# A planner's transfer times, the places of its loads, and a lag: one re-plan of a fused attention and FFN kernel

## The chip, the cores and the metric

The kernel runs on one core of a Trainium2 chip. The metric is the device time of one launch in microseconds. TensorE (PE), VectorE (DVE), ScalarE (ACT) and GpSimd (POOL) compute; SyncE (SP) issues most of the DMAs, POOL those of the FFN weights.

## What is computed

Forgetting attention for 8 batches of 8 heads (576 tokens, head size 64), and a SwiGLU block on its output. All inputs and the output are float32; the kernel computes its matrix products in bf16.

```python
scores = scale * np.matmul(q, k.transpose(0, 1, 3, 2))
cum = np.cumsum(np.log(np.clip(f, 0.0001, 1.0)), axis=-1)
decay = cum[:, :, :, None] - cum[:, :, None, :]
scores = np.where(causal, -1000000000.0, scores + decay)
attn = softmax(scores)
x = np.matmul(attn, v)          # to tokens x 512
g = x @ w_gate                  # 512 x 1536
out = (g * sigmoid(g) * (x @ w_val)) @ w_out
```

## The kernel before, in words

**Work.** Attention goes by pairs of heads: 32 pairs, four to a batch. A pair's queries come in nine blocks of 64 rows. Blocks 0 to 3 are group g = 0, blocks 4 to 8 are g = 1. For each pair: k and q are loaded (L325; two slots each, kf and qf), cast to bf16 on POOL (kb at L352, qb at L350), transposed on PE (L364) into one of two PSUM banks "tx", and copied out by ACT or DVE (L378, L380) to kt and qz. The cumulated log gates of the two heads, cb, are loaded from DRAM (L332, five slots). PE makes the scores in one of two banks "sp" (L399, with a mask at L403), DVE adds cb and takes the row minimum (L415), ACT takes exp with the row sum (L429), DVE inverts the sums (L445, L447; ACT may do the first step, L443), and POOL normalizes into the packed tile pk (L464). Then P is transposed into pT: for pairs 0 to 7 on PE (L488, with copies out at L493), for pairs 8 to 31 by a transposing DMA issued by SP (L476): one of 19 blocks for g = 1, one of 6 for g = 0. P times V (L514) goes to a "tx" bank, and ACT or DVE copies it into xT (L538), a ring of 2560 tokens.

**FFN.** Tokens go in tiles of 256, 256, seven times 512, 256, 256. Per tile and unit of 512 columns: gate and value products (L595, banks "gv"), tanh on ACT (L601), two DVE operations (L603, L606) to hh. Then the output product (L620; one bank "op"; in groups of four matmuls, three groups for 128 tokens), its eviction to ot by ACT (L630) or DVE (L632), and the store (L637).

**What sets the order.** Nothing is ordered by hand. The code makes a list of operations, each with the engines that may run it and a cost in ns on each, what it reads and writes, a due time `prio`, and for a DMA its transfer time `dma`. `Plan.order` then runs a list scheduler on this model: again and again it takes the operation that can start first (ties: smaller `prio`), on the engine where this holds, and books the engine. It gives one fixed order for each engine; on the chip every queue runs in that order, and each instruction waits for its own data and buffers. A wrong cost gives no wrong result, but an order that doesn't fit. Three things matter here:

- *Due times.* `ORDER` numbers the units (pair, group): first the eight of pairs 0 to 3, then two for each later pair, g = 1 before g = 0. `first[p]` is the pair's first number, s. Casts and transposes of a pair are due at s - 1, a transposing DMA at its own unit's number - 1, the loads of k and q at s.
- *Turns.* The tiles of a buffer pool or PSUM bank are handed out in a fixed sequence, sorted by the due time of the operation that first writes them, or by a `turn` of its own. P·V has such a turn in the "tx" banks: its number plus `LAG`, for pairs 0 to 3 plus `EASE`.
- *Transfers.* The plan has one wire for the queues of SP (with ACT) and one for POOL's. A transfer starts at the later of the wire's end and 600 ns after the issue, takes `dma` (more where both wires run), and has landed 1200 ns later. `after` holds a load back in the plan until another operation is done; on the chip there is no such wait.

The first 40 or so loads, weights among them, follow a list of their own (`STARTUP`).

Of the kernel before, what the change touches and what calls it, by code (L numbers as in the profile page):

```python
# [13 lines left out]

BIG = 1.0e9
HUGE = 3.0e38


class Op:
    __slots__ = ("n", "engs", "fn", "reads", "writes", "prio", "lat", "dma", "deps", "start", "end", "eng", "after", "holds", "bias")  # L20

    def __init__(self, n, engs, fn, reads, writes, prio, lat, dma, after, holds):
        self.holds = list(holds)
        self.n, self.engs, self.fn, self.reads, self.writes = n, engs, fn, reads, writes
        self.prio, self.lat, self.dma, self.after = prio, lat, dma, after
        self.start = self.end = self.eng = None
        self.bias = {}


class Plan:  # L30
# [23 lines left out]
    def order(self):  # L54
# [22 lines left out]
        left = {k: len(v) for k, v in users.items()}  # L77
        until = {k: 0 for k in users}
        slots = {name: [None] * len(b) for name, b in self.pools.items()}
        free = {e: 0 for e in ("PE", "DVE", "ACT", "POOL", "SP")}  # L80
        wire = {True: 0, False: 0}
        ready = {o.n: 0 for o in self.ops if not waiting[o.n]}
        done = []
# [22 lines left out]
        while ready:  # L106
            best = None
            for n, r in ready.items():
                o = self.ops[n]
                got = room(o)  # L110
                if got is None:
                    continue
                for e, dur in o.engs.items():
                    s = max(r, got[0], free[e])
                    c = (s + o.bias.get(e, 0), o.prio, n, e, dur, got[1])
                    if best is None or c[:4] < best[:4]:
                        best = c
            if best is None:
                raise RuntimeError("no operation can start: " + ", ".join(str(self.ops[n].writes) for n in list(ready)[:20]))
            s, _, n, e, dur, take = best  # L120
            o = self.ops[n]
            s -= o.bias.get(e, 0)
            for k, b in take:
                name = self.home[k]
                self.where[k] = b
                slots[name][b] = k
                taken[name] += 1
            o.start, o.eng = s, e
            free[e] = s + dur
            if o.dma:  # L130
                q = e == "POOL"
                at = max(wire[q], free[e] + 600)
                both = max(0, min(2 * o.dma, wire[not q] - at))
                wire[q] = at + o.dma + both / 2
                wire[not q] += both / 2
                o.end = wire[q] + 1200
            else:
                o.end = free[e] + o.lat
            for k in {*o.writes, *o.reads, *o.holds}:
                left[k] -= 1  # L140
                until[k] = max(until[k], o.end)
            del ready[n]
            for kid in kids.get(n, ()):
                waiting[kid.n] -= 1
                if not waiting[kid.n]:
                    ready[kid.n] = max(d.end for d in kid.deps)
            done.append(o)
# [10 lines left out]
def kernel(  # L158
# [41 lines left out]
    AHEAD = 8  # L200
    BEHIND = 5
    BOTH = 8
    LAG = 3.5
    EASE = (2.5, 3)
    SPARE = {"ACT": 300, "DVE": 600}
    EARLY = {0: 4.3, 1: 7.8}
    FREE = 8
    STARTUP = "p0 f9 f0 p1 c1 p2 c2 p3 v00 c3 v01 wg0 wv0 wg2 wv2 v02 v03 v04 wg4 wv4 wg8 wv8 p4 c4 wo0 p5 c5 wo4 wo8 p6 c6 v10 v11 v12"
    ORDER = [(p, g) for g in range(2) for p in range(NPB)]
    ORDER += [(p, g) for p in range(NPB, NPAIR) for g in (1, 0)]  # L210
# [84 lines left out]
    def gates(key, parts, np_, prio):  # L295
        x = lambda: pl.buf(key)[0:np_, :]
        for n, (a, z, src) in enumerate(parts):
            loads["f", key, n] = pl.op({"SP": 600}, lambda e, a=a, z=z, src=src: nc.sync.dma_start(out=pl.buf(key)[a:z, :], in_=src),
                                       (), [(key, 0)] + [key] * (n == 0), prio + n * .01, dma=500)
        pl.op({"DVE": 460}, lambda e: nc.vector.tensor_scalar(x(), x(), 1.0e-4, 1.0, op0=ALU.max, op1=ALU.min),  # L300
              [(key, 0)], [(key, 1)], prio, holds=[key])
        pl.op({"ACT": 690}, lambda e: nc.scalar.activation(x(), x(), AF.Ln), [(key, 1)], [(key, 2)], prio, holds=[key])
        pl.op({"DVE": 1350}, lambda e: nc.vector.tensor_tensor_scan(x(), tiny[0:np_, 0:1].to_broadcast((np_, S)), x(), 0.0, ALU.mult, ALU.add),
              [(key, 2), "tiny"], [(key, 3)], prio, holds=[key])
# [3 lines left out]
    for p in range(NDIRECT):  # L308
# [1 line left out]
        gates(("cb", p), [(64 * h, 64 * h + 64, fall[2 * p + h:2 * p + h + 1, :].to_broadcast((64, S))) for h in range(2)],  # L310
              P, -99.9 + 3 * p)
    pl.op({"SP": 600}, lambda e: nc.sync.dma_start(out=cum_dram, in_=pl.buf("fa")[:BH, :]),
          [("fa", 3)], ["cum_dram"], -120, dma=500, lat=0, holds=["fa"])
    pl.op({"ACT": 1400}, lambda e: nc.scalar.activation(tiny[:, 1:2], tiny[:, 0:1], AF.Exp), [(("cb", NDIRECT - 1), 2), ("fa", 2), "ln"], ["exp"], -95)

    def half(key):
# [3 lines left out]
    def load_pair(p):  # L320
        b, hp = divmod(p, NPB)
        s = first[p]
        for name, src, pr in (("k", k, 0), ("q", q, .1)):
            pl.key((name + "f", p), name + "f")
            loads[name, p] = pl.op({"SP": 620} if p else {"ACT": 620}, lambda e, name=name, src=src: (nc.scalar if e == "ACT" else nc.sync).dma_start(  # L325
                out=pl.buf((name + "f", p))[0:ROWS[name][0], :, :],
                in_=src[b, 2 * hp:2 * hp + 2].rearrange("h (p r) d -> p h (r d)", r=ROWS[name][1])),
                (), [(name + "f", p)], (-99 + 3 * p if p < NPB else s) + pr, dma=1130 if name == "k" else 980, after=[sums[p - 3, 0 if p - 3 >= NPB else 1]] if p >= NPB else [])
        if p >= NDIRECT:
            pl.key(("cb", p), "cb")  # L330
            for h in range(2):
                loads["cb", p, h] = pl.op({"SP": 600}, lambda e, h=h: nc.sync.dma_start(  # L332
                    out=pl.buf(("cb", p))[64 * h:64 * h + 64, :],
                    in_=cum_dram[2 * p + h:2 * p + h + 1, :].to_broadcast((64, S))),
                    ["cum_dram"], [("cb", p), (("cb", p), 3)], -98.5 + 3 * p if p < NPB else s + .2, dma=560)

    def prepare(p):
        s = first[p]
# [96 lines left out]
    def normalize(p, g):  # L435
# [37 lines left out]
        tk = ("pT", p, g)  # L473
        pl.key(tk, f"pT{g}")
        if (p, g) not in ON_PE:
            pl.op({"SP": 550 + 150 * NSL[g]}, lambda e: nc.sync.dma_start_transpose(  # L476
                out=pl.buf(tk), in_=pl.buf(kk).rearrange("p s k -> p (s k)")),
                [kk], [tk], s - 1, dma=186 * NSL[g])
            return
        for a in range(0, NSL[g], 8):  # L480
            z = min(a + 8, NSL[g])
# [62 lines left out]
    def load_v(b):  # L544
        for c in range(5):
            n = min(P, S - P * c)
            fk = ("vf", b, c)
            pl.key(fk, "vf")
            s = c * .5 - 97 * (c < 2) + 1
            if b:  # L550
                s = at[b * NPB, 1] + c * .1 - .5
            wait = [sums[b * NPB - 2 + (c > 2), 0 if b > 1 else 1]] if b else []
            loads["v", b, c] = pl.op({"SP": 620}, lambda e, c=c, n=n, fk=fk: nc.sync.dma_start(
                out=pl.buf(fk)[0:n, :, :], in_=v[b, :, P * c:P * c + n, :].rearrange("h p d -> p h d")),
                (), [fk], s, dma=1500 * n / P, after=wait)
            def cast(e, c=c, n=n, fk=fk):
                (nc.scalar.copy if e == "ACT" else eng[e].tensor_copy)(pl.buf(("vt", b))[0:n, c, :, :], pl.buf(fk)[0:n, :, :])  # L557
            o = pl.op({"POOL": 670} if b else {"POOL": 670, "ACT": 580, "DVE": 600}, cast,
                  [fk] + ([("z", "vt", b)] if c == 4 and b < 2 else []), [("vt", b), ("vt", b, c)], s + .5)
            o.bias = SPARE  # L560


    def weights():
# [4 lines left out]
        for a, z in zip(cuts, cuts[1:]):  # L568
            for nm, wt, src in (("wg", wg, moe_w_gate), ("wv", wv, moe_w_val)):
                piece({"POOL": 600}, lambda e, wt=wt, src=src, a=a, z=z: nc.gpsimd.dma_start(  # L570
                    out=wt[:, :, a:z], in_=src[:, a:z].rearrange("(ko p) n -> p ko n", p=P)),
                    (), [(nm, n) for n in range(a // P, z // P)], 2 + a / 256, dma=4.7 * (z - a) + 900)
        for c in range(0, KF, 4):
            piece({"POOL": 600}, lambda e, c=c: nc.gpsimd.dma_start(
                out=wo[:, c:c + 4, :], in_=moe_w_out[c * P:(c + 4) * P, :].rearrange("(ko p) n -> p ko n", p=P)),
                (), [("wo", n) for n in range(c, c + 4)], 7 + c / 4, dma=3300)

    gates_of = {}

# [29 lines left out]
    def project(t, tok, n):  # L609
        nf = 512 // n  # L610
        for ms in range(n // P):
# [15 lines left out]
            for a, z in ((0, DM // 2), (DM // 2, DM)) if end else ((0, DM),):  # L627
# [6 lines left out]
                if end:  # L634
# [1 line left out]
                pl.op(engs, evac, [bk], [ok, (ok, a)], pr - 5000)  # L636
                pl.op({"SP": 560}, lambda e, ms=ms, ok=ok, a=a, z=z: nc.sync.dma_start(  # L637
                    out=out[tok + ms * P:tok + ms * P + P, a:z], in_=pl.buf(ok)[:, a:z]),
                    [(ok, a)], [("out", t, ms, a)], pr - 5000, dma=680 * (z - a) // DM, lat=0, holds=[ok])

    for p in range(NPAIR):
        load_pair(p)
# [76 lines left out]
```

## Time and profile before

| | us |
|---|---|
| median of 3 runs | 436.98 (436.26 to 438.55) |
| profiled execution | 437.73 |
| its span, first to last instruction | 436.0 |
| PE busy | 402.5 (92%), 3192 matmuls |
| DVE busy | 347.9 (80%) |
| ACT busy | 302.8 (69%) |
| POOL busy | 252.1 (58%) |
| SP's DMA queue q1 | 71.9% of 16 engines' span, 66.57 MB |
| POOL's DMA queue q0 | 7.1%, 4.72 MB |

The granted TensorE clock is 1.0 in all 40 slices of the span. "Busy" is the union of an engine's instructions; matmuls overlap, so a PE that is busy all the time need not be at its peak. The wait rows name an instruction, what it waited for, the total in us, how often, and the longest. SP issues DMAs and computes nothing; a long SP instruction is an issue that took long.

### The profile page before, as it was taken

The page shows a single profiled execution, that of the slowest core. Times are in us where ns is not written, and L with a number is a line of the kernel's source. Part 1 is how long each engine was busy: PE and PEld are TensorE (multiplying, and loading weights), DVE is VectorE, ACT ScalarE, POOL GpSimd, SP SyncE. Part 2 cuts the span into 40 slices and gives each one's busy share as a digit, 9 for nine tenths or more (in the row PEclk, how much of TensorE's full clock was granted, in tenths as well). Part 3 has the DMA queues.
Part 4 walks back from the last instruction along what each step waited for, and adds up shares of the span by engine and source line. Part 5 has one row for each costly group of instructions (what it writes and reads, how often), then busy time and mean ns, then how long its engine had stood idle before and what let it go on. Part 6 is the DMA issues. An engine that isn't in the chain of part 4 may idle for free.

```text
span 436.0 us, 9859 instructions
## 1 busy us (share of the span) xinstructions
PE 402.5 (92%) x3192; PEld 229.2 (53%) x3192; DVE 347.9 (80%) x1081; ACT 302.8 (69%) x848; POOL 252.1 (58%) x452
## 2 busy tenths in 40 slices
PE   2578999998999998989999999999999999999996
PEld 1436777755454454444555554555445444457662
DVE  6788799798999798977999998999989665365340
ACT  6799789989877968776798777677678633232321
POOL 5699748748956855886668768938875600000000
PEclk9999999999999999999999999999999999999999
DMA  7999999637978998999999999999994640010112
GB/s 195 212 188 227 203 207 215 165 101 212 192 169 187 225 215 188 194 218 234 198 207 213 222 219 206 189 223 207 202 199 100 117 108 26 24 50 24 50 50 72
DMA packets 143956, 72.51 MB, mean 166 GB/s; under 512 B 118560, under 2 KB 130592, under 8 KB 143904
## 3 DMA queue, kind: packets, MB, share of 16 engines
q1 hardware_dynamic: 137732, 66.57, 71.9%
q0 software_dynamic: 5808, 4.72, 7.1%
q10 hardware_dynamic: 364, 0.59, 0.6%
q8 instruction: 25, 0.41, 0.4%
q14 instruction: 27, 0.22, 0.2%
HBM read 47.33 MB, written 9.58 MB: 131 GB/s over the span
## 4 chain that ended last, share of the span: by engine, by line
PE 60%; DVE 12%; DMA 10%; ACT 9%; POOL 4%; issue 4%; SPq 1%; DVEq 0%; ACTq 0%; POOLq 0%
PE gv L595 29%; PE op L620 15%; DMA qf<-in_q_dram 7%; PE sp L399 5%; DVE t L415 4%; PE tx L514 4%; ACT eo L429 3%; ACT e L429 2%; PE tx L364 2%; DVE qz L380 2%; DVE th L603 2%; POOL pk L464 2%; DMA pT<-pk 2%; PE gv L620 2%; DVE hh L606 2%
## 5 line engine op out<-in xcount | busy, mean ns | idle before, releaser
L415 DVE CUSTOM_DVE_ANT_0 t<-sp,cb 128x512 f32<-128x512 f32 (+7 forms) x288 | 130.4, 476 | 12.2 <-PE sp L403 5.9
L464 POOL TENSOR_SCALAR pk<-e,lr 128x512 bf16<-128x512 f32 (+3 forms) x186 | 97.7, 529 | 33.3 <-DVE tm L415 17.6
L595 PE MATMUL gv<-xT,wv 128*128 128x512 bf16 (+1 forms) x528 | 111.2, 340 | 0.2 <-DVE th L603 0.2
L595 PE MATMUL gv<-xT,wg 128*128 128x512 bf16 (+1 forms) x528 | 111.2, 340 | 0.2
L601 ACT ACTIVATE th<-gv 128x512 f32<-128x512 f32 x108 | 64.1, 594 | 61.0 <-PE gv L595 59.7
L603 DVE SCALAR_TENSOR_TENSOR th<-th,gv 128x512 f32<-128x512 f32 x108 | 73.9, 684 | 37.5 <-ACT th L601 37.1
L429 ACT ACTIVATE e<-t,tm 128x448 f32<-128x448 f32 (+4 forms) x160 | 88.8, 556 | 20.2 <-DVE tm L415 19.6
L620 PE MATMUL op<-wo,hh 128*128 128x512 bf16 x396 | 100.7, 379 | 2.1 <-DVE ot L632 1.3
L606 DVE TENSOR_TENSOR hh<-th,gv 128x512 bf16<-128x512 f32 x108 | 73.4, 685 | 10.3 <-PE op L620 4.1
L399 PE MATMUL sp<-kt,qz 128*128 128x448 bf16 (+4 forms) x320 | 72.3, 294 | 9.2 <-DVE tm L415 8.1
L429 ACT ACTIVATE eo<-t,tm 128x256 f32<-128x256 f32 (+3 forms) x128 | 71.2, 556 | 6.4 <-DVE tm L415 6.0
L595 PEld LDWEIGHTS <-wg 128*128 128x128 bf16 x528 | 48.9, 98 | 37.1 <-issue 0.2
L464 POOL TENSOR_SCALAR pk<-eo,lr 128x128 bf16<-128x128 f32 (+3 forms) x123 | 65.3, 531 | 2.5 <-ACT th L601 1.0
L595 PEld LDWEIGHTS <-wv 128*128 128x128 bf16 x528 | 47.8, 98 | 34.9 <-issue 0.3
L620 PEld LDWEIGHTS <-hh 128*128 128x128 bf16 x432 | 39.6, 98 | 41.8 <-issue 2.3
L403 PE MATMUL sp<-mask,ident 128*128 128x64 bf16 x288 | 48.1, 197 | 0.0
L399 PEld LDWEIGHTS <-qz 128*128 128x128 bf16 x320 | 30.6, 100 | 24.5 <-DVE qz L380 2.7
L350 POOL TENSOR_SCALAR qb<-qf 72x1024 bf16<-72x1024 f32 x31 | 32.9, 1062 | 14.8 <-DMA qf<-in_q_dram 7.2
L352 POOL CAST kb<-kf 96x768 bf16<-96x768 f32 x31 | 25.4, 820 | 27.4 <-DMA kf<-in_k_dram 19.3
L403 PEld LDWEIGHTS <-ident 128*128 128x128 bf16 x288 | 27.0, 100 | 21.3 <-issue 11.0
L557 POOL CAST vt<-vf 128x512 bf16<-128x512 f32 (+1 forms) x40 | 24.3, 608 | 17.4 <-DMA vf<-in_v_dram 17.2
L514 PE MATMUL tx<-pT,vt 128*64 128x320 bf16 (+4 forms) x448 | 29.7, 266 | 1.5 <-ACT e L429 0.5
(61 smaller groups left out, 393.2 us busy)
## 6 DMA issues: line engine op xcount, KB each, us to landing
out_dram<-ot SPq DMA_DIRECT2D x35, 256.0 KB, 2.4
kf<-in_k_dram SPq DMA_DIRECT2D x31, 288.0 KB, 6.3
qf<-in_q_dram SPq DMA_DIRECT2D x31, 288.0 KB
cb<-cum_f SPq DMA_DIRECT2D x62, 144.0 KB, 4.7
vf<-in_v_dram SPq DMA_DIRECT2D x32, 256.0 KB, 4.4
wo<-in_moe_w_out_dram POOLq DMA_DIRECT2D x3, 512.0 KB, 9.9
vf<-in_v_dram SPq DMA_DIRECT2D x8, 128.0 KB
wg<-in_moe_w_gate_dram POOLq DMA_DIRECT2D x2, 512.0 KB, 9.1
```

The costliest lines, as they stand in the source:

```text
L350: eng[e].tensor_scalar(dst, src, -scale, 1.0, op0=ALU.mult, op1=ALU.mult)
L399: nc.tensor.matmul(sp[:, o:o + z - a], qz[:, i, :, :].rearrange("p h r -> p (h r)"), kt[:, a:z], start=True, stop=not last)
L403: nc.tensor.matmul(sp[:, o - QB:o], ident, mask, start=False, stop=True)
L415: nc.vector.tensor_tensor_reduce(out=pl.buf(tk)[:, a:z], in0=pl.buf(sk)[:, o:o + z - a], in1=pl.buf(("cb", p))[:, a:z], scale=1.0, scalar= ...
L429: nc.scalar.activation(pl.buf(ek)[:, :L], pl.buf(tk)[:, :L], AF.Exp, bias=pl.buf(("tm", p, g))[:, i:i + 1], scale=-1.0, accum_out=pl.buf(( ...
L464: eng[e].tensor_scalar(dst, src, r, 1.0, op0=ALU.mult, op1=ALU.mult)
L514: nc.tensor.matmul(xo[r, 0:QB * n], vt[:, c, 2 * hp + h, :], pT[:, a:a + n, 64 * h:64 * h + 64], start=(c == 0), stop=(c == nch - 1))
L595: nc.tensor.matmul(pl.buf(bk)[:, j * n:j * n + n], wt[:, ko, fc * P:fc * P + P], xT[:, ko, x0:x0 + n], start=ko == 0, stop=ko == KD - 1)
L601: pl.op({"ACT": 487}, lambda e, u=u: nc.scalar.activation(pl.buf(("th", t, u)), pl.buf(("wg", t, u)), AF.Tanh, scale=0.5), [("wg", t, u)], ...
L603: pl.op({"DVE": 605}, lambda e, u=u: nc.vector.scalar_tensor_tensor(pl.buf(("th", t, u)), pl.buf(("th", t, u)), 1.0, pl.buf(("wg", t, u)), ...
L606: pl.op({"DVE": 605}, lambda e, u=u: nc.vector.tensor_mul(pl.buf(("hh", t, u)), pl.buf(("th", t, u)), pl.buf(("wv", t, u))), [("u", t, u), ...
L620: nc.tensor.matmul(pl.buf(bk), hh[:, (fc % nf) * n + ms * P:(fc % nf) * n + ms * P + P], wo[:, fc, :], start=fc == 0, stop=fc == KF - 1)
```

## The change

It alters the plan's model and due times:

- engines are free from 700 ns on, and PE costs double before 25 us (`COLD`);
- a transfer starts 2000 ns (POOL: 2550) after the start of its issue, and has landed 1100 ns after the wire's end; a transposing DMA (`ring`) holds SP until 1450 ns before its wire's end;
- the `dma` times of all loads and stores, and SP's cost of a transposing DMA, get other values;
- loads of k, q and cb of pairs 4 and up are due `SOON` = 6 numbers before s, those of v 6 before the first unit of their batch (before: 0.5); loads of k and q are held back until the exponentials of the pair four before, not three; cb gets such a hold of its own;
- `LAG` goes from 3.5 to 4.5.

Numbers of buffers, the work and the turns' rule stay. Cut to its core:

```diff
-        free = {e: 0 for e in ("PE", "DVE", "ACT", "POOL", "SP")}
+        free = {e: 700 for e in ("PE", "DVE", "ACT", "POOL", "SP")}
...
+            if e == "PE" and s < COLD:
+                dur *= 2
...
-                at = max(wire[q], free[e] + 600)
+                at = max(wire[q], s + (2550 if q else 2000))
                 both = max(0, min(2 * o.dma, wire[not q] - at))
                 wire[q] = at + o.dma + both / 2
                 wire[not q] += both / 2
-                o.end = wire[q] + 1200
+                if o.ring:
+                    free[e] = max(free[e], wire[q] - 1450)
+                o.end = wire[q] + 1100
...
-    LAG = 3.5
+    LAG = 4.5
...
+    SOON = 6
+    BACK = 4
+    CBACK = 4
...
-                (), [(name + "f", p)], (-99 + 3 * p if p < NPB else s) + pr, dma=1130 if name == "k" else 980, after=[sums[p - 3, 0 if p - 3 >= NPB else 1]] if p >= NPB else [])
+                (), [(name + "f", p)], (-99 + 3 * p if p < NPB else s - SOON) + pr, dma=1060, after=[sums[p - BACK, 0 if p - BACK >= NPB else 1]] if p >= NPB else [])
...
-                    ["cum_dram"], [("cb", p), (("cb", p), 3)], -98.5 + 3 * p if p < NPB else s + .2, dma=560)
+                    ["cum_dram"], [("cb", p), (("cb", p), 3)], -98.5 + 3 * p if p < NPB else s - SOON + .2, dma=570, after=[sums[p - CBACK, 0 if p - CBACK >= NPB else 1]] if p >= NPB + 1 else [])
...
-            pl.op({"SP": 550 + 150 * NSL[g]}, lambda e: nc.sync.dma_start_transpose(
+            pl.op({"SP": 300 + 153 * NSL[g]}, lambda e: nc.sync.dma_start_transpose(
                 out=pl.buf(tk), in_=pl.buf(kk).rearrange("p s k -> p (s k)")),
-                [kk], [tk], s - 1, dma=186 * NSL[g])
+                [kk], [tk], s - 1, dma=500 + 118 * NSL[g]).ring = True
...
-                s = at[b * NPB, 1] + c * .1 - .5
+                s = at[b * NPB, 1] + c * .1 - SOON
...
-                (), [fk], s, dma=1500 * n / P, after=wait)
+                (), [fk], s, dma=1460 if n == P else 800, after=wait)
```

Smaller ones: loads of f and the store of the cumulated gates 500 to 570, weight pieces `4.7 * (z - a) + 900` to `5.1 * (z - a) + 880` and 3300 to 3500, stores of the output 680 to 950.

## The prediction

> **What bounds the kernel now.** I read the page's busy shares first, then busy time by stretch, then the waits of TensorE, then the chain of waits, and last the timeline of single loads.
>
> ```profile
> core 0: us, PE busy (x) PEld busy (x) DVE busy (x) ACT busy (x) POOL busy (x), PEclk, DMA share, GB/s
> 0.00:50.00 50.00, 31.47 (x316) 23.02 (x316) 38.54 (x129) 40.77 (x109) 40.20 (x85) 1.00 1.03 203
> 50.00:110.00 60.00, 56.11 (x600) 39.41 (x595) 52.66 (x181) 54.15 (x148) 40.55 (x69) 1.00 0.80 181
> 110.00:340.00 230.00, 223.09 (x1738) 115.63 (x1736) 211.59 (x697) 177.45 (x534) 166.28 (x289) 1.00 1.00 200
> 340.00:436.00 96.00, 91.83 (x547) 51.09 (x545) 45.09 (x79) 30.40 (x60) 5.11 (x10) 1.00 0.21 57
> ```
>
> Busy time by stretch: PE is idle for 18.53 us of the first 50, for 3.89 of the next 60, for 6.91 between 110 and 340, and for 4.17 at the end. In the long middle three things are nearly full at once: PE 97%, DVE 92%, and the DMA engines (share 1.00). After 340 only FFN is left and PE has no holes until the last output. The amount of work is the same after the change, so the change can only fill PE's holes. Its whole field is the 10.8 us after 50 us (somewhat more, since the modelled end of a matmul, some 0.17 us beyond its place in the stream, covers short holes) and a part of the start-up.
>
> ```profile
> PE tx L364 <- POOL qb L350: 1.9, 3, 1.1
> PE sp L399 <- DVE tm L415: 1.7, 4, 0.9
> PE op L620 <- DVE ot L632: 1.3, 3, 0.6
> PE op L620 <- DVE hh L606: 0.4, 1, 0.4
> ```
>
> Waits of PE between 110 and 340 us (total, times, longest): 1.9 us for a q cast that came late, and 3.4 us for DVE in the three other rows.
>
> ```profile
> 47.26 5.98 DMA qf<-in_q_dram
> 53.31 14.76 DMA qf<-in_q_dram
> ```
>
> The chain of waits, in order of time: the loads of q for pairs 5 and 6. They have equal size, yet the second takes 14.76 us against 5.98: POOL issues two pieces of the output weights at 54.33 and 55.13, and they flow beside it.
>
> **The change, part by part.** No instruction is added or removed. Costs, due times and the plan's idea of a DMA change, and so the order on every queue and some choices of engine. What follows compares the two built orders. The sum is made on the profiled execution (437.73 us, span 436.0), 0.75 above the median of 436.98; differences carry over.
>
> *A, pair 6.* POOL's new order casts k of pair 7 before it issues the last two pieces of wo (before: after them). The load of that k moves up in SP's queue from behind the load of q 6 to five places ahead of it, where two cb loads of about equal size stood. It needs the slot that the cast of k 5 frees at 49.4, so it lands at about 56 (6.3 us, the median of these loads), the cast takes 0.82, and wo goes out 2 to 3 us later, out of q 6's way. PE is idle for 1.43 us in 60 to 70, of which 0.47 waits directly for this q. Value -1.0; bounds -1.43 and +4 (second rival). The Trainium skill, "DMA: Bandwidth & Descriptors", section "Issuing engines are not separate DMA queues", says that DMAs of all queues run on the same 16 engines and interleave, so what q 6 gains wo would lose. The 14.76 us agree with it. By it alone this term is 0 and the sum below -2.5.
>
> *B, first FFN tile with 512 tokens.* LAG 4.5 moves the PSUM bank's turn for the second P·V (g = 0) of pairs 4 to 7 behind the transposes of k and q three pairs on. For later pairs 3.5 and 4.5 give the same order, since no other turn lies between them. The tile's first matmul (103.19 us) waits for pair 7. In the new order it stands behind five more score groups of pair 9 and the transposes of pair 10. The DVE work moved ahead of it is 5 x 0.56 (L415 and its accumulator row) + 2 x 0.75 (L380), less one output eviction of 0.69: 3.6 us, the upper bound. Some 1.4 us of it is PE work that must be done anyway (scores and transposes), and it falls into a stretch in which PE has holes: 2.46 us between 90 and 110, all of which gone is the lower bound. Done early, the DVE work is missing later, where DVE is 92% busy. Value +1.0.
>
> *C, VectorE.* The new plan gives six net output evictions, two net xT evictions and one of pT more to ACT:
>
> ```profile
> L632 DVE TENSOR_SCALAR ot<-op 128x512 f32<-128x512 f32 x12 | 8.3, 691 | 1.4 <-PE op L620 0.9
> L538 DVE CAST xT<-tx 128x320 bf16<-128x320 f32 (+1 forms) x31 | 13.8, 455 | 2.8 <-PE tx L514 2.6
> ```
>
> Third column, mean ns: 6 x 0.691 + 2 x 0.455 + 0.55 = 5.6 us less on DVE. The 38 k and q evictions that change sides cancel. ACT is at 77% in the middle and takes the work without being asked for time. PE's DVE waits there are 3.9 us in all (the three rows above, 0.5 in smaller ones). Bounds -5.6 (DVE as the true limit) and 0 (another DVE operation is late next). Value -2.5, somewhat under the middle.
>
> *D, loads of pairs.* The words say "ahead of the transposes of P". The built SP queue says otherwise for the middle. Between pairs 11 and 31, q was issued behind the second transposing DMA of the pair three before it for 5 pairs (14, 16, 21, 22, 29); now for 12 (16, 19 to 24, 26, 27, 28, 30, 31), and k for 10 instead of none. SOON does go ahead, but the slots (two for kf, two for qf) and the plan's new ring rule hold the loads back. What such a q costs shows in the timeline:
>
> ```profile
> 164.49 0.50 SPq L325 DMA_DIRECT2D qf<-in_q_dram  x1
> ...
> 169.64 0.43 PE L364 MATMUL tx<-ident,qb 72*128 72x72 bf16 x8 [1.14 <-POOL qb L350]
> ```
>
> Pair 16: 5.15 us from the issue of q to its transposes, and PE waits 1.14 us. Such a q leaves SP 1.9 us after the transposing DMA of its neighbour (1.24 + 0.6), so the transposes of q are ready 7.0 us after it. P·V, which uses that transposing DMA, starts 2.7 to 7.5 us after it in the trace (median 4.5 of 21 pairs). PE thus needs 2.5 us of other work between P·V and the transposes (4.3 at the earliest P·V). I count it in the new PE order, with 0.865 per group of four matmuls, 0.2 per score group and 0.26 per transpose group. For the 12 pairs it is 4.1, 2.4, 3.0, 4.3, 9.3, 1.7, 6.8, 3.5, 2.6, 3.7, 3.5 and 2.6 us (the old plan had 1.1 to 2.4 for most pairs): the new plan knows that q is late and puts FFN there. At the median it is 0.9 us short in all, at the earliest P·V 11.6. The 1.94 us of the old waits after 110 (three in the row above) go. Value 0.9 - 1.94 = -1.0; bounds -1.94 and +9.7.
>
> *E, start-up.* SP's first 21 issues are the same, and before 50 us elementwise work is the limit (DVE, ACT and POOL 77 to 82% busy). The doubled PE costs before 25 us swap a few neighbours. Value 0, bounds +-1.7 (the longest PE wait there, 1.68).
>
> Sum: -1.0 + 1.0 - 2.5 - 1.0 = -3.5: 434.2 on the profiled execution, **433.5** on the median.
>
> **Rivals.**
> 1. *Bigger gain.* DMA is nearly empty between 90 and 100 us (share 0.27), while SP waits 6.7 us for an output eviction. In the new queue the loads of pair 10 stand ahead of that output. If this and all of C count: -1.43 - 1.0 - 5.6 - 1.9 gives 427. Against it: the next loads stand behind the second output, which is not done sooner.
> 2. *Slower, wo and tile 2.* Pieces of wo took 12.5 us from 52 to 70. Issued at 56.8 they land at 69.3, and the second projection group of tile 0 stood at 70.96. If k 7 drags as q 6 did (at 61.6, say), PE, in fixed order, stands 4 us; with B at its upper bound: +4 + 3.6 - 2.5 - 1.0 gives 441. It decides from k 7 landing 1.5 us later than 56.
> 3. *Slower, loads just in time.* D at its upper bound: -1.0 + 1.0 - 2.5 + 9.7 gives 444. It decides where P·V starts under 4 us after its transposing DMA; 9 of the 21 pairs did.
> 4. *It does not do what it says.* The loads have two slots and DMA is full, so lead can't grow, C is eaten by the next late DVE operation, and the holes only move: 437. The Trainium skill, "Perfetto Trace Analysis", section "Identifying Performance Opportunities", says that the same gap repeating can mean too few buffers for the next tile. By it priorities give nothing and the time stays; the trace has such a gap at L364 (three rows of it in the middle), but not on most pairs.
>
> **How the numbers follow.** Forecast 0.45, rival 1 0.12, rival 2 0.13, rival 3 0.10, rival 4 0.20. Half a percent, about what a measurement of this kernel can tell from no change, is 2.2 us: faster means under 434.8. The forecast's own spread (431 to 436) lies for three quarters under that. With rival 1 this is 0.46; slower is rivals 2 and 3 with an edge of 4, 0.25; the rest 0.29. Range 427 to 443, from rival 1 to just short of rival 3.
>
> **What would show it.** A: the load of q 6 under 12 us, PE idle in 60 to 70 under 0.7. B: the first 512-wide gate matmul between 102 and 106 us. C: L632 with about 6 counts on DVE, DVE busy 342 us, PE's waits for DVE between 110 and 340 under 2 us. D: waits of L364 for qb under 1.5 us in the middle. E: PE busy in 0 to 50 within 1.7 of 31.5. Wrong would be: PE idle in the middle above 9 us (D or a new DVE wait), or a wait of L620 for wo's DMA.

## The result and the profile after

| | before | changed |
|---|---|---|
| median of 4 runs each, on one chip | 437.76 (436.26 to 439.01) | 442.50 (441.71 to 442.96) |
| ratio, 95% interval | 1 | 1.0108 (1.0068 to 1.0147) |
| profiled execution, span | 437.73, 436.0 | 441.71, 439.9 |

The changed kernel is 1.1% slower; 433.5 had been forecast. Lines of its code stand nine further down than before (L415 is L424, L632 is L641).

Busy time by stretch of the changed kernel:

```profile
core 0: us, PE busy (x) PEld busy (x) DVE busy (x) ACT busy (x) POOL busy (x), PEclk, DMA share, GB/s
0.00:50.00 50.00, 31.24 (x266) 21.61 (x267) 33.90 (x122) 40.17 (x105) 37.69 (x83) 0.93 0.97 184
50.00:110.00 60.00, 54.33 (x593) 40.64 (x598) 48.89 (x160) 50.96 (x134) 37.41 (x61) 0.97 0.91 186
110.00:340.00 230.00, 223.16 (x1724) 117.47 (x1752) 209.45 (x692) 178.15 (x544) 164.32 (x288) 1.00 1.01 202
340.00:440.00 100.00, 95.11 (x568) 52.83 (x576) 50.45 (x102) 35.84 (x78) 10.18 (x20) 1.00 0.21 57
```

Read the first row with care. PE's busy time is that of before (31.24 against 31.47), but with 266 matmuls instead of 316 (267 weight loads instead of 316 say the same): the clock column says 0.93, and a matmul at half clock is busy for longer. Two equal score matmuls of the changed kernel, ahead of a fall of the clock and in it:

```profile
35.20 0.38 PE L408 MATMUL sp<-kt,qz 128*128 128x512 bf16 x1 [1.12 <-DVE tm L424]
38.59 0.59 PE L408 MATMUL sp<-kt,qz 128*128 128x512 bf16 x1 [0.16 <-DVE tm L424]
```

DVE shows the loss plainly: up to 110 us it did 33.90 + 48.89 = 82.8 us of work, before it was 91.2. The page's row of the clock places the falls:

```profile
PEclk9996999998999999999999999999999999999999
```

The trace's records of the granted clock give 0.5 from 36.4 for 6.8 us and from 104.6 for 3.4 us; before, it was 1.0 from 26.9 us to the end of the work. Those records begin at 29.5 and 26.9 us. The 1.0 that the views give for the time ahead of them is not a record: in the kernel before, such a score matmul took 0.59 us at 24.47 and 0.38 at 28.74, so its start was slow too.

Waits of PE between 110 and 340 us, and the rows of the output eviction (L641) and of xT (L547):

```profile
PE sp L408 <- DVE tm L424: 2.4, 8, 0.5
PE sp L408 <- ACT qz L387: 0.8, 2, 0.6
PE gv L604 <- DVE th L612: 0.6, 1, 0.6
```

```profile
L547 DVE CAST xT<-tx 128x256 bf16<-128x256 f32 (+1 forms) x29 | 12.9, 444 | 4.0 <-PE tx L523 3.8
L641 DVE TENSOR_SCALAR ot<-op 128x512 f32<-128x512 f32 x6 | 4.1, 689 | 0.5 <-PE op L629 0.4
```

No wait for a q cast is left in the middle (1.9 us before), and DVE has six output evictions instead of twelve. So the signs that had been forecast for the middle came. To see where the time went, take the moment at which PE has done an equal amount of its planned work (its matmuls weighted by their lengths), and subtract that of before. All kernels of the experiments that matter are in the same table; each column comes from one profiled execution:

| at this time of before | changed | model alone (five) | loads alone (six) | all but the model (nine) | changed, old start rule (eleven) | the same, no ring rule (fifteen) | changed, three places undone by hand (fourteen) |
|---|---|---|---|---|---|---|---|
| 38.3 | +4.0 | +4.0 | +0.6 | -0.4 | +0.6 | -0.4 | +2.3 |
| 58.6 | +3.7 | +3.5 | +0.6 | -0.4 | -0.2 | -1.1 | +2.3 |
| 91.3 | +5.1 | +3.7 | +2.1 | +0.4 | +0.4 | +0.9 | +5.6 |
| 103.8 | +8.5 | +6.5 | +5.3 | +1.3 | +1.2 | +1.7 | +8.3 |
| 135.9 | +7.4 | +5.7 | +4.4 | +0.4 | -0.1 | +0.5 | +7.2 |
| 191.6 | +4.6 | +3.6 | +1.7 | -1.5 | -2.4 | -1.2 | +4.5 |
| 244.0 | +3.1 | +23.1 | +1.4 | -2.2 | -3.5 | -2.4 | +3.0 |
| 348.2 | +4.5 | +23.5 | -1.6 | -1.9 | -4.1 | -1.3 | +4.1 |
| 418.4 | +4.5 | +27.5 | -0.7 | -1.8 | -1.5 | -1.2 | +4.1 |
| first 512-wide gate matmul (before 103.2) | 113.3 | 109.9 | 110.1 | 105.0 | 104.9 | 105.5 | 113.2 |
| DVE busy to 110 us (before 91.2) | 82.8 | 83.1 | 87.4 | 90.3 | 91.7 | 91.1 | 83.9 |

The changed kernel loses 4.0 us before 40 us, 1.1 more up to 91 and 3.4 more ahead of the first 512-token tile. It wins back 5.4 us from there to 244, and loses 1.4 later.

### The profile page after: what moved, and what is told of

Same layout as the page of the kernel before. It is cut to its first block, busy times and chain, and to the rows that moved or that the text cites. A ratio compares the mean times of both kernels' runs of the same rounds, so it can differ in the third digit from the quotient of the medians.

```text
span 439.9 us, 9779 instructions
## 1 busy us (share of the span) xinstructions
PE 403.8 (92%) x3143; PEld 232.6 (53%) x3192; DVE 342.7 (78%) x1073; ACT 305.1 (69%) x858; POOL 249.6 (57%) x450
## 4 chain that ended last, share of the span: by engine, by line
PE 66%; DVE 11%; ACT 7%; DMA 5%; issue 4%; POOL 2%; DVEq 0%; POOLq 0%; SPq 0%; ACTq 0%
PE gv L604 33%; PE op L629 14%; PE sp L408 7%; DVE t L424 6%; PE tx L523 5%; DMA wo<-in_moe_w_out_dram 3%; PE tx L373 2%; ACT eo L438 2%; ACT e L438 2%; DMA kf<-in_k_dram 2%; PE gv L497 2%; PE gv L629 2%; DVE qz L389 2%; PE sp L412 1%; DVE th L612 1%
## 5 line engine op out<-in xcount | busy, mean ns | idle before, releaser
L424 DVE CUSTOM_DVE_ANT_0 t<-sp,cb 128x512 f32<-128x512 f32 (+7 forms) x288 | 130.1, 476 | 12.0 <-PE sp L412 3.0
L473 POOL TENSOR_SCALAR pk<-e,lr 128x256 bf16<-128x256 f32 (+3 forms) x182 | 96.2, 532 | 62.3 <-DVE lr L456 26.0
L604 PE MATMUL gv<-xT,wv 128*128 128x512 bf16 (+1 forms) x515 | 109.0, 340 | 1.3 <-DVE th L612 0.6
L612 DVE SCALAR_TENSOR_TENSOR th<-th,gv 128x512 f32<-128x512 f32 x108 | 73.7, 682 | 40.5 <-ACT th L610 40.2
L629 PE MATMUL op<-wo,hh 128*128 128x512 bf16 x376 | 97.2, 379 | 4.4 <-DMA wo<-in_moe_w_out_dram 2.0
L408 PE MATMUL sp<-kt,qz 128*128 128x64 bf16 (+6 forms) x317 | 73.6, 300 | 13.6 <-DVE tm L424 10.6
L473 POOL TENSOR_SCALAR pk<-eo,lr 128x128 bf16<-128x128 f32 (+3 forms) x125 | 66.5, 533 | 4.7 <-DVE lr L456 4.1
L604 PEld LDWEIGHTS <-wv 128*128 128x128 bf16 x528 | 48.8, 98 | 38.3 <-issue 1.3
L389 DVE COPY qz<-tx 64x576 bf16<-64x576 bf16 x41 | 30.8, 752 | 7.1 <-ACT qz L387 4.7
L639 ACT ACTIVATE ot<-op 128x512 f32<-128x512 f32 x27 | 16.0, 594 | 22.3 <-PE op L629 22.2
```

The source lines that it names most:

```text
L389: nc.vector.tensor_copy(dst, src)
L408: nc.tensor.matmul(sp[:, o:o + z - a], qz[:, i, :, :].rearrange("p h r -> p (h r)"), kt[:, a:z], start=True, stop=not last)
L424: nc.vector.tensor_tensor_reduce(out=pl.buf(tk)[:, a:z], in0=pl.buf(sk)[:, o:o + z - a], in1=pl.buf(("cb", p))[:, a:z], scale=1.0, scalar= ...
L473: eng[e].tensor_scalar(dst, src, r, 1.0, op0=ALU.mult, op1=ALU.mult)
L604: nc.tensor.matmul(pl.buf(bk)[:, j * n:j * n + n], wt[:, ko, fc * P:fc * P + P], xT[:, ko, x0:x0 + n], start=ko == 0, stop=ko == KD - 1)
L612: pl.op({"DVE": 605}, lambda e, u=u: nc.vector.scalar_tensor_tensor(pl.buf(("th", t, u)), pl.buf(("th", t, u)), 1.0, pl.buf(("wg", t, u)), ...
```

## The experiments

Each comes with its ratio to the kernel before, measured on the same chip (95% interval). "Changed" has 1.0108 (1.0068 to 1.0147), from four executions of each kernel. The changed kernel was not measured again beside the runs; so they are compared with it by these ratios, and where the intervals meet, a gain over it is not shown.

**One: fill PE in the start-up.** Three matmuls more (`KEEP` is 3), results unused, behind each score bank of group 1 of pairs 0 to 2.

```diff
+                for _ in range(KEEP if p < 3 and g == 1 else 0):
+                    nc.tensor.matmul(pl.pools["op"][0][:, 0:256], ident, kt[:, 0:256], start=True, stop=True)
```

> The changed kernel, order and all, with three extra matmuls of 256 columns behind each score bank of pairs 0 to 2, g = 1 (15 x 3, into the output-product bank, which is overwritten before its first use; no result depends on them). Theory of places: the changed kernel lost 4.0 us by 42 us, half of it because PE's granted clock fell to 0.5 from 36.4 to 43.2 us after a stretch with holes. With the holes filled the clock stays 1.0 there, the first gate matmul comes at about 39.7 instead of 41.7, and the time is 442.5 - 2 = 440.5. Rival (the clock only shows idleness and costs nothing, or the whole loss is late loads): the extra 45 x 0.107 = 4.8 us of PE work lies in PE's way: 442.5 to 445.

442.08, ratio 1.0081 (1.0054 to 1.0107). The fall of the clock in the start-up was gone (1.0 from 29.1 to 104.2 us). So holes had caused it. But the first gate matmul came at 42.4, against 41.8 in the changed kernel and 39.7 expected: the fall is not what made the start late. By the ratios the gain is 1.2 us, with intervals that overlap; 4.8 us of work were added.

**Two: weights first.** In the plan the cast of k of pair 7 waits for the last piece of wo; PE's, DVE's and ACT's orders stay.

```diff
+    casts["k", 7].after.append(loads["wo", 8])
```

> The changed kernel with one more tie in the plan: POOL's cast of k for pair 7 comes after the last piece of wo is issued, as before the change. PE, DVE and ACT orders are those of the changed kernel; POOL differs from its 80th operation, SP from its 45th. Theory of places: PE's 2.0 us wait for wo's DMA (L629) goes and the loss of 1.1 us at 80 to 90 us of the progress curve with it: 441.4; the load of q for pair 6 goes back above 12 us and PE waits up to 0.5 us for it. Rival (what wo gains q 6 loses, as the same 16 DMA engines carry both): 442.5 within 0.5.

441.81, ratio 1.008 (1.0056 to 1.0105). The wait for wo fell from 2.0 to 0.8 us, and the load of q 6 took 15.0 us from issue to cast instead of 11.4. About 1 us again, with intervals that overlap those of the changed kernel.

**Three: LAG back to 3.5** in the changed kernel.

> The changed kernel with LAG 3.5 again; PE's order is the same up to its 129th operation. Theory of places: LAG put the first 512-token tile behind pair 9's scores and cost 3.3 us there (clock fall at 104.6 us included): with LAG back the first 512-wide gate matmul comes at about 110 instead of 113.3, no clock fall near 105, and the time is 439.5 to 440. Rival (late loads of q cost the time, and this order has 14 of them against 12): 442.5 or more.

445.42, ratio 1.0146 (1.0113 to 1.0179): no gain, a loss if anything. The theory that the lag had moved the first 512-token tile, and that this was the loss, fell here: the tile began at 111.7 and PE still waited 2.6 us for DVE's sums between 88 and 114 us (2.8 in the changed kernel).

**Four: LAG 4.5 alone** in the kernel before.

> The kernel before with LAG 4.5 alone; PE's order is the same as before up to its 126th operation, so the start is untouched. Theory of places: first 512-wide gate matmul 3 us later (106 instead of 103.2), part of it regained by attention being ahead: 438 to 441 against 437.8. Rival (late loads; here 7 late q against 5): no change, 437.5 to 438.5.

447.68, ratio 1.0222 (1.0172 to 1.0271). PE's waits from 98 to 125 us:

```profile
PE tx L370 <- POOL qb L356: 5.4, 1, 5.4
PE sp L405 <- DVE tm L421: 3.3, 7, 1.0
PE tx L370 <- POOL kb L358: 2.3, 1, 2.3
```

The lag puts the transposes of pair 10 ahead of the tile, and with the old due times k and q of pair 10 are not there yet (7.7 us). The clock stood at 0.5 from 105.1 for 17.1 us. LAG is harmful here only without the early loads, as run nine shows.

**Five to eight: one part of the change each, in the kernel before.** The model (five); the due times and holds of loads (six); SOON alone (seven); the doubled PE cost before 25 us alone (eight). Each is the full diff with the other edits left out.

> The changed plan with its new model of transfers (start offsets, ring, doubled PE cost before 25 us, dma values), but the old due times of loads (no SOON, BACK, CBACK) and LAG 3.5. Theory (places and clock: the loss sits in the start-up, which the model re-plans, and before the first 512-token tile, which LAG and the early loads re-plan; holes of PE there lower the granted clock): start-up as in the changed kernel, first gate matmul at 41 to 42.5 with a fall of the clock near 37 to 44; before the 512-token tile a small gap only (3 score groups of pair 9 and none of pair 10's transposes stand ahead of it), no long fall near 105; 440.5 to 443. Rival (loads late for the transposes are what costs; 17 q loads stand behind a transposing DMA here, 12 in the changed kernel, 5 before): 445 or more, with waits of the transposes for qb of over 5 us in the middle.

> The old plan with the new due times of loads alone (SOON 6, BACK 4, CBACK 4; old model, LAG 3.5). Theory (places and clock): start-up as before (first gate matmul within 0.5 us of 37.6), but 7 score groups of pair 9 and 2 transpose groups of pair 10 stand ahead of the first 512-token tile (before: 2 and 0), so PE waits for DVE there, the clock falls near 105 for over 6 us, and the time is 443 to 448. Rival (late loads are what costs; none is late here): 436 to 438, and at most 0.5 us of waits for qb in the middle.

> The old plan with SOON 6 alone (loads of k, q, cb and v due six numbers sooner; holds, model and LAG as before). Theory (places and clock): the order up to the first 512-token tile is that of before, so its start is within 1.5 us of 103.2 and the clock stays 1.0 from 27 us on; in the middle 1 late q instead of 5 saves under 2 us: 436 to 438.5, not to be told from before. Rival (early loads cost by themselves, since DMA is full): slower by 2 us or more.

> The old plan with the doubled PE cost before 25 us alone. Theory A (this doubling is what re-planned the start-up): first gate matmul at 40 us or later, a fall of the clock between 36 and 44, no fall near 105, 440 to 442. Theory B (the start-up's loss comes from the new start offsets of transfers instead): first gate matmul within 1 us of 37.6, no fall, 437 to 438.5.

| | us | ratio |
|---|---|---|
| model alone | 465.19 | 1.06 (1.0581 to 1.0619) |
| loads alone | 438.35 | 0.998 (0.9952 to 1.0007) |
| SOON alone | 439.32 | 0.9999 (0.9971 to 1.0026) |
| doubled PE cost alone | 437.79 | 0.9977 (0.9954 to 0.9999) |

This turned the question around. The early loads cost nothing in all: they lose 5.3 us up to the first 512-token tile, as expected, and have it all back by 276 us, which I had not expected (443 to 448 was the forecast, 436 to 438 its rival). The doubled PE cost is innocent too. The model alone has the changed kernel's start-up (+4.0 at 38 us), and then one disaster that the changed kernel is spared. SP and PE of that run:

```profile
239.70 4.07 SPq L482 DMA_TRANSPOSE pT<-pk  x1
243.83 1.56 SPq L643 DMA_DIRECT2D out_dram<-ot  x2
245.49 4.21 SPq L482 DMA_TRANSPOSE pT<-pk  x2
249.81 1.28 SPq L559 DMA_DIRECT2D vf<-in_v_dram  x2
251.18 1.28 SPq L482 DMA_TRANSPOSE pT<-pk  x1
252.51 0.57 SPq L331 DMA_DIRECT2D kf<-in_k_dram  x1
```

```profile
PE tx L370 <- POOL kb L358: 12.6, 1, 12.6
```

Four transposing DMAs, two outputs and two loads of v stand ahead of the k that PE needs next; the clock was 0.5 from 247.4 for 17.1 us. The model wants the early due times with it. My rival (waits for qb over 5 us) had the right queue and the wrong tensor: qb cost 1.4 us.

**Nine to eleven: combinations.** All but the model (nine); loads, with the weights first as in run two (ten); the changed kernel with only the start rule put back (eleven):

```diff
-                at = max(wire[q], s + (2550 if q else 2000))
+                at = max(wire[q], free[e] + 600)
...
-                o.end = wire[q] + 1100
+                o.end = wire[q] + 1200
```

> Everything but the model: the old plan with SOON 6, BACK 4, CBACK 4 and LAG 4.5. Theory (the net loss is the model's re-planned start-up plus a gap before the first 512-token tile; the early loads repay 5 to 6 us in the middle): start as before (+0.6 at most), 3 score groups of pair 9 ahead of the tile instead of 7 with the early loads alone, so the gap there is 2 to 4 us, the middle repays 5 to 6: 433 to 437. Rival (LAG 4.5 costs by itself, as it did alone with 9 us): 441 or more.

> The old plan with SOON 6, BACK 4, CBACK 4 (old model, LAG 3.5), and in the plan the cast of k of pair 7 waits for the last piece of the output weights. Against the early loads alone: no wait for those weights (1.5 us there), 2 score groups of pair 9 ahead of the first 512-token tile instead of 7 (a gap of 3.2 us there). Theory (gap and wait are lost for good): 432 to 435.5. Rival (what is lost there comes back in the middle anyway, since DVE is the limit from 110 to 340): 437 to 439.

> The changed kernel with the old rule of a transfer's start and landing (600 ns after the end of the issue, landed 1200 ns after the wire's end); all else changed, with 11 late q loads. Theory (the rule of the start re-plans the start-up, and this costs the first 4 us): first gate matmul within 1 us of 37.6, no fall of the clock before 100, and 435 to 439. Rival (dma values and the ring rule cost it): first gate matmul at 40 or later, 441 to 444.

| | us | ratio |
|---|---|---|
| all but the model | 436.34 | 0.9969 (0.9933 to 1.0004) |
| loads, weights first | 438.39 | 0.999 (0.9951 to 1.003) |
| changed, old start rule | 437.80 | 0.9951 (0.9922 to 0.9981) |

Two lines of the model are the whole loss: with the old start rule the rest of the change is not slower but 0.5% faster. One expectation missed: the clock did fall before 100 us, to 0.5 at 34.0 for 3.4 us. Run ten was the rival's: the gap before the tile went (first gate matmul at 105.0 instead of 110.1), and the time stayed. Busy time by stretch of run eleven, its end at 434:

```profile
0.00:50.00 50.00, 32.17 (x318) 23.85 (x319) 39.45 (x132) 40.46 (x105) 41.23 (x88) 0.97 0.97 201
50.00:110.00 60.00, 55.50 (x591) 39.53 (x598) 52.27 (x177) 53.69 (x151) 41.06 (x69) 1.00 0.88 191
```

318 matmuls and 39.45 us of DVE by 50 us, against 266 and 33.90.

**Twelve: fill PE before the first 512-token tile.** Every score matmul of pairs 8 and 9 of the changed kernel is done twice into the same bank.

```diff
-                for i, a, z in bank:
+                for i, a, z in bank * (2 if p in TWICE else 1):
                     last = z == QB * (i + 1)
+                    o = 0 if (i, a, z) == bank[0] else o
```

> The changed kernel with every score matmul of pairs 8 and 9 done twice into the same bank (the second overwrites the first), in the same order: some 0.2 us of PE work more for each of the 10 groups ahead of the first 512-token tile, where PE waits for DVE. Theory (holes lower the clock; the clock then stretches the 25 transposes and P times V behind them): no fall of the clock near 105, the tile's first gate matmul 0.5 to 1.5 us sooner than 113.6, 441 to 442.5. Rival (DVE alone sets the pace there and the clock costs nothing): the tile not sooner, the time the same or up to 1 us more.

441.82, ratio 1.0049 (1.0025 to 1.0073). No fall near 105. The tile began at 113.9, after a start-up that was 1.3 us later in that profile: some 0.7 us sooner by that count (113.3 in the changed kernel), at the edge of what can be told. By the ratios the run is 2.6 us under the changed kernel, with intervals that just overlap.

**Thirteen and fourteen: places of the start-up undone by hand** in the changed order. What they undo is seen in DVE's timeline, of before and then of the changed kernel (start, duration, engine, line; in brackets the idle time ahead and who ended it):

```profile
16.00 0.18 DVE L447 RECIPROCAL lr<-lr 128x4 f32<-128x4 f32 x1
16.09 0.73 DVE L380 COPY kt<-tx 128x576 bf16<-128x576 bf16 x1
17.13 0.42 DVE L415 CUSTOM_DVE_ANT_0 t<-sp,cb 128x256 f32<-128x256 f32 x1 [0.31 <-DMA cb<-cum_f]
```

```profile
17.20 0.18 DVE L456 RECIPROCAL lr<-lr 128x4 f32<-128x4 f32 x1 [0.93 <-ACT lr L452]
19.08 0.76 DVE L389 COPY qz<-tx 64x576 bf16<-64x576 bf16 x1 [1.70 <-ACT qz L387]
19.87 0.42 DVE L424 CUSTOM_DVE_ANT_0 t<-sp,cb 128x256 f32<-128x256 f32 x1
```

Before, DVE copies out k 3 and goes on to the sums of pair 1 at 17.13. In the changed order ACT, the fullest engine there (4.94 of 5 us at 20 to 25 before), has the copy of k 3 and the first step of pair 0's inverse sums, and DVE's copy of q 3 stands ahead of the sums of pair 1: they start 2.7 us later. Run thirteen moves that copy behind them; fourteen also gives the two others back to DVE.

```diff
+        by("ACT", "kt", 3).eng = "DVE"
+        by("ACT", "lr", 0, 0).eng = "DVE"
+        o = by("DVE", "qz", 3)
+        line.remove(o)
+        line.insert(line.index(by("DVE", "t", 1, 1)) + 1, o)
```

> The changed order with one operation moved by hand: DVE's copy of pair 3's q stands behind the four score sums of pair 1 (as in the kernel before), not ahead of them; all else on every queue as in the changed kernel. Theory (in the changed order this copy waits 1.7 us for q 3, while the sums of pair 1 behind it could start at 17.1 instead of 19.9, and from there the whole start-up is late): sums of pair 1 start at 17 to 17.5, first gate matmul 39 to 40.5 instead of 41.7, 439.5 to 441.5. Rival (ACT is the limit of the start-up; one copy on DVE changes nothing): 442 to 443.

> As the run with one copy moved by hand, and the copy out of k 3 and the first step of the inverse sums of pair 0 done by DVE instead of ACT, as in the kernel before; all else as in the changed kernel. Theory (these three places are the start-up's loss): first gate matmul 38 to 39.5, the start-up's fall of the clock gone or at most 3.4 us, 438 to 440 (the rest of the loss, before the first 512-token tile, stays). Rival (the loss is spread over many places of the start-up): first gate matmul after 40.5, 441 to 443.

441.67, ratio 1.006 (1.0025 to 1.0095), and 440.38, ratio 1.0039 (1.0009 to 1.0069). In thirteen's profile the first gate matmul came at 42.3 (expected 39 to 40.5): a miss, in an execution in which DVE's copy of k 2 was already 1.1 us late (14.68 against 13.61). In fourteen the sums of pair 1 started at 17.14 and the first gate matmul at 40.3 instead of 41.8, between the theory (38 to 39.5) and the rival (after 40.5). That is about a third of the start-up's loss, and in the profiled execution it did not last. PE's waits for wo, in the changed kernel (two rows) and then in fourteen:

```profile
66.62 1.02 PE L629 MATMUL op<-wo,hh 128*128 128x512 bf16 x3 [1.24 <-DMA wo<-in_moe_w_out_dram]
74.64 1.02 PE L629 MATMUL op<-wo,hh 128*128 128x512 bf16 x3 [0.71 <-DMA wo<-in_moe_w_out_dram]
66.17 1.20 PE L629 MATMUL op<-wo,hh 128*128 128x512 bf16 x4 [2.19 <-DMA wo<-in_moe_w_out_dram]
```

The first piece of wo is issued behind the cast of k 6. It went out at 56.2 us instead of 56.6 and landed at 66.1 instead of 66.6, so PE waited a microsecond longer for it; the clock fell again at 66.9 us. Between 60 and 70 us the DMA engines are full (share 1.18). The load of q 6 took 16.0 us, and its cast began 3.9 us later than in the changed kernel, but PE waited only 0.2 us for it. By 91 us this execution was as late as the changed kernel. It was one of the run's slower ones (441.36): by the ratios the run is 3.0 us under the changed kernel, with intervals that just touch. Whether the three places are worth nothing or some 3 us is therefore open.

**Fifteen and sixteen.** Run eleven without the ring rule, so that no q load stands behind the transposing DMA of the pair three before (11 did); and run nine with the weights first.

> The changed kernel with the old rule of a transfer's start, and without the rule that a transposing DMA holds SP: the order of e11 at first, but no q load stands behind a transposing DMA of the pair three before it (e11: 11). Theory (a late q load costs little where the plan knows of it): within 1.5 us of e11's 437.8. Rival (late loads cost what my third rival said): 2 to 5 us faster than e11, 433 to 436.

> Everything but the model (as e9, 436.3), and in the plan the cast of k of pair 7 waits for the last piece of the output weights. e9 waits once for them, 1.1 us. Theory (that wait is on the path): 434.5 to 436, 1 us under e9. Rival (the time comes back before the first 512-token tile, where PE waits for DVE anyway): 436 to 437.5, no gain.

434.81, ratio 0.993 (0.9907 to 0.9953), and 437.78, ratio 0.9965 (0.9934 to 0.9997). The first is the best kernel here, 0.7% faster than before; its interval overlaps that of run eleven, so eleven late q loads cost 3 us at the most and perhaps nothing. (The medians lie 3.0 us apart, in the rival's range; the ratios, each taken on its own chip, 0.9.) The second gained nothing over nine.

## Why the prediction was wrong

**E, the start-up, is the step that failed.** It read: value 0, bounds +-1.7, "the doubled PE costs before 25 us swap a few neighbours". The bound was a wait of PE (1.68 us at 21; two waits for the first loads are longer, 4.80 and 2.06). It came to +4.0. PE was not the limit there, as E itself had said (elementwise work is): two operations moved onto ACT, the fuller engine, and one copy placed ahead of four sums cost 2.7 us on DVE before 20 us. With these three undone (run fourteen) the sums start on time, and a third of the delay of the first gate matmul goes; which places make up the rest is open. It also blamed the wrong edit: the doubled costs alone gave +1.4 at 38 us, gone by 71 (run eight); the start rule gave the rest (run eleven). In the book that the plan keeps (not measured), the changed kernel's plan has cb of pair 1 landed at 17.2 and the copies of q 3 starting at 16.9; the old one has 14.3 and 14.5. The chip in the kernel before: cb at 17.1, ACT's copy of q 3 at 18.0. The new rule is right about cb and an us too early with q 3, so it puts them in the wrong order; the old rule is wrong by some 3 us on both and has the order right. That this one order is why the new rule loses is argued from the book; that the rule loses is shown. And E's own test was blind: "PE busy in 0 to 50 within 1.7 of 31.5" came true at half clock. Counts of matmuls or DVE's busy time would have shown it.

The miss in terms of the sum, read at 418 us: -3.5 had been forecast, +4.5 came, 8.0 us apart. E has 4.0 of it, A and B together 4.5 (8.5 at 103.8 less E's 4.0; they had been put at 0), and from 104 to 348 us, the stretch of C and D, 4.0 were won instead of 3.5.

**B, the first 512-token tile, was mis-sized.** I said +1.0, bounded by 3.6, first matmul at 102 to 106. It came at 113.3. Of the 10.1 us, 5.1 are inherited from what lies before and 3.4 arise there (just inside the bound); the rest is work done ahead. The cause was not LAG as I had it: with LAG 3.5 PE still waited 2.6 us for DVE there (run three), and with LAG 4.5 and a good start-up the tile began at 105.0 (run nine). Nor was it the place of the weights: with them first (run two) 3.1 us still arose, though with the loads alone that had closed the gap (run ten). With the old start rule (run eleven) it was 0.8. What in the new order makes the gap stays open. The better sign is DVE's work up to 110 us, the last row of the table: it is low where the tile is late. That the tile waits for pair 7 and the pairs go at DVE's pace fits this, but no run shows it by itself.

**A turned into the second rival, at a smaller price.** "If k 7 drags as q 6 did (at 61.6, say)": its cast began at 61.3. The chain of waits of the changed kernel:

```profile
53.01 8.15 DMA kf<-in_k_dram
...
62.08 12.52 DMA wo<-in_moe_w_out_dram
```

This too is E's: the slot for k 7 came free at 53.0 us, where A had counted on 49.4 (at 58.6 us the run was 3.7 behind); and the load took 8.2 us instead of 6.3. q 6 did come sooner (11.4 us from issue to cast instead of 14.9), and wo later: PE waited 2.0 us for it, which the prediction had named as a sign of being wrong. PE idle in 60 to 70 us was 1.29 us, not under 0.7. But only 0.7 of the 2.0 us was for a piece behind the cast of k 7, where the rival had 4. The other 1.2 was for the first piece, behind the cast of k 6, issued at 56.6 us instead of 51.0. The Trainium skill, "DMA: Bandwidth & Descriptors", section "Issuing engines are not separate DMA queues", had an answer in the prediction: transfers of all queues interleave on the same engines. Three traces agree: q 6 took 14.9 us beside the last two pieces of wo (before), 11.4 with these issued 3.6 us behind it (changed), and 15.0 beside them again (run two). Run fourteen does not: 16.1 us, with the pieces issued 3.2 us behind it. So sharing with wo is not all that sets this time. That the rival's 441 lies near the measured 442.5 is luck: it had 0 for E.

**The signs of C and D came.** DVE 342.7 us (342 forecast), six evictions, no wait for qb in the middle; rival three did not happen. Only PE's waits for DVE there were 3.2 us (3.9 before) instead of under 2. From 104 to 244 us the changed kernel won back 5.4 us, where C and D had 3.5 together. How much of it is C, how much D and how much mere catching up was not separated: the loads alone won back 3.9 there. C's part is doubtful: with the loads alone DVE has ten output evictions and is busy for 346.4 us, in run eleven it has twelve, as before, and 349.9 us (347.9 before), and these two won back 6.9 and 5.3 us from 104 to 348, more than the changed kernel's 4.0. Run eleven, where the start-up is sound, ends 1.5 us under the kernel before in its profile; -3.5 had been the sum with a cost of 1.0 for B in it.

**The clock** had no term in the sum. How much of the 4.5 us is its own stays open: with the first fall removed by extra work (run one) the gain was 1.2 us by the ratios, with the second removed (run twelve) 2.6, at the edge of the intervals. A short fall need not cost much: runs eight, eleven and sixteen had one of 3.4 us in the start-up and were not slower than the kernel before.

## What to carry to other kernels

A list scheduler that decides by who can start first is not made better by a number that is more exact by itself: what counts is the order of events, and here two times wrong by about the same amount gave a better order than one right and one wrong. Edits of a planner lean on each other (the model alone +6%, with the early loads and the lag +1.1%; the lag alone +2.2%, with the early loads nothing), so test them in combination and with one left out. Where elementwise engines set the pace, compare counts of instructions and their busy time by stretch, not PE's busy share, and bound a re-plan by their slack, not by PE's longest wait.

## What the runs showed of the hardware

*Holes that no single wait shows lower the clock.* Cut each trace into stretches of 3.41 us, in step with the clock's records, and take the share in which PE computes or loads weights. At full clock, up to 425 us of each run, all 13 stretches under 49% were followed by a fall to 0.5, of the 23 between 49 and 65% eight were, of the 2009 above that none (18 profiles of this kernel and its variants). The longest single hole in the stretches ahead of the changed kernel's two falls (52 and 47% busy) was 1.10 and 1.19 us. Falls lasted 3.4, 6.8, 10.2 or 17.1 us. The Trainium skill, "TensorE: Matmul & The Clock Gate", Part 1, states a free-running window of 3413 ns after which the clock halves or returns; the lengths agree, all near multiples of it. Its advice to avoid idle gaps of over about 3 us (section "Why this matters for your kernels") would not have warned of these two falls: gaps of 1.2 us are enough when there are several.

*The same order starts differently.* The start-ups of the changed kernel and of run twelve hold the same operations in the same order, and the fall there lasted 6.8 and 10.2 us, in one profiled execution each.
